# Attention with sinks and a sliding window, then a gated feed-forward layer: sink keys and the neighbouring half tile scored by separate 64-wide matmuls, sink values placed by small DMAs, casts and masks open to several engines

## The chip, the cores and the metric

The kernel runs on one core of one Trainium2 chip. The metric is the device time of one execution in microseconds (us); several executions give a median. Five engines work side by side and meet only through semaphores: PE (TensorE, matmul and transposes), DVE (VectorE), ACT (ScalarE), POOL (GpSimd, which here also issues the loads) and SP (SyncE, which here issues stores, DMA transposes and, in the changed kernel, small copies inside on-chip memory).

## What is computed

Inputs are float32; four batches, eight heads, 768 tokens, 64 features per head. Heads 0, 2 and 6 ("retrieval") attend causally to all earlier tokens. Heads 1, 3, 4, 5 and 7 ("streaming") see only the first four tokens (the sinks) and the last 64.

```python
scores = (1/8) * q @ k.T                       # per batch and head
keep   = causal                                # retrieval heads
keep   = causal & (key < 4 | query - key < 64) # streaming heads
a      = softmax(where(keep, scores, -1e9)); attn = a @ v
x      = attn, heads side by side              # 3072 tokens x 512
h      = gelu(x @ w_gate) * (x @ w_val)        # 512 -> 1536
out    = x + sigmoid(x @ w_res) * (h @ w_out)  # 1536 -> 512
```

## The kernel before

**Chunks.** The 3072 tokens are taken in six chunks of 512 tokens, four query tiles of 128 each. With six tiles to a batch, chunk 0 is tiles 0 to 3 of batch 0; chunk 1 is tiles 4 and 5 of batch 0 with tiles 0 and 1 of batch 1; chunk 2 is tiles 2 to 5 of batch 1; chunks 3, 4 and 5 repeat this for batches 2 and 3. Chunks 1 and 4 therefore handle two short segments with twice as many, but half as wide, casts and evictions. Each chunk runs three steps: `attention`, `gate_value`, `output`. The output of a chunk is interleaved with the attention of the next, so the program alternates between an "attention stage" (attention of chunk c with the output of chunk c-1) and a "gate/value stage" (96 matmuls of 512 columns). The last output stands alone at the end.

**Keys and queries.** They are needed with features on partitions. For batch 0 and for tiles 0 to 5 of batch 1 (chunks 0, 1, 2) `loads_rows` fetches them by large row loads from POOL (L410), transposes them on PE (L504) and evicts them alternately on DVE and ACT (L512) into `qkt`. From chunk 3 on `loads_natural` fetches them in 64 KB pieces into the staging tile `qks` and SP transposes them by DMA (L534). Two heads share 128 partitions, so one matmul has 64 contraction rows, and two heads' matmuls can run beside each other in the two row halves of PE. There are two buffers each of `qks`, `qkt`, `va` and `vs`.

**Sinks.** A streaming head needs, for query tile i, its own tile ("diag"), and of the tile ahead of it only the second half of the keys, plus the four sinks ("prev"). So `key_sinks` (L459 to L474) makes a copy `kts` of the keys of each tile (L465), then overwrites its first four columns by the sink keys (L468); `values` makes the same copy `vs` of the values (L449) and overwrites its first four rows (L452). All four copies are DVE work. One matmul of 128 keys by 128 queries then scores sinks and window together (L602, `kts` operand), and one weighs both (L668, `vs` operand).

**Attention.** Per pair of heads: `scores` (L602) fills PSUM banks `pb` of 512 columns; `exps` takes the exponential on ACT (L613) into `er` or `es` and multiplies masks `m_causal`, `m_diag`, `m_prev` on DVE (L641); `weigh` multiplies by the values (L668; a column of ones gives the sum), takes the reciprocal (L675) and normalises into `xtok` (L678), both DVE. When both heads of a group of 128 features (`cb`) are done, `to_features` casts it to 16 bits on DVE (L689), transposes it on PE (L693) and evicts it on DVE (L697) into `xT`.

**Gate, value, output.** `gate_value` makes 12 groups of 4 + 4 matmuls over the four `cb` (L731); every one of them depends on all of `xT`. ACT takes the gelu (L735), DVE forms h (L737). `output` makes, for each of four token tiles, 4 matmuls by `wr` (L753), 12 by `wo` (L758), a tanh on ACT (L761, in place of the sigmoid), a multiply on DVE (L763), an add of x on POOL (L767; on DVE in the last chunk) and a store on SP (L773). ACT holds either the exponential's or the gelu's table and loads it anew at each change (ACT_TABLE_LOAD).

**What sets the order.** The kernel's Python holds a list of tasks with an engine, an estimated duration, dependencies and a priority (1000 per chunk, then offsets). `Graph.schedule` (L122) simulates the engines with these estimates and fixes each engine's order for good: at each moment a free engine takes its ready task of lowest priority number. `assign_waits` and `emit` turn the dependencies into semaphores. Engines then work strictly in that order, so a late task holds back what stands behind it on its engine. PSUM has eight banks: two for weighted values, six shared by scores (`scr`, at most 4) and feed-forward (`moe`, at most 4).

## Time and profile before

| what | value |
|---|---|
| median of 3 runs | 323.49 us (321.61 to 324.11) |
| the profiled execution | 323.42 us, of which the span of the profile is 321.7 |
| TensorE clock granted, mean | 0.963 of full |
| busy: PE, DVE, ACT, POOL | 283.0, 177.9, 141.8, 106.2 us |
| matmuls | 2096, 88% of the span busy |
| gelu / exponential table loads | 12 of some 1.28 us |

The span is a single profiled execution from its first to its last instruction; what lies around it is 1.7 us. A row of the grouped view reads: line of the kernel, engine, operation, written tile <- read tiles, shapes, number of times | busy us, mean ns of one | idle time of the engine just ahead of them and what ended it. A row of the chain of waits reads: start, duration, engine, tile and line; it follows the work that ended last back from the end. A row of the stage table reads: stretch in us, its length, then busy time and number of instructions of PE, of its weight loads (PEld), of DVE, ACT and POOL, then the granted PE clock, the DMA share and GB/s. Matmul durations overlap, since they are pipelined; spacing between starts says more than the duration of one.

### The profile page before, as it was taken

Reading aid. Unit: us, or ns where it says so; the run is one execution under the profiler, and the core shown is the slowest. Engines: PE = TensorE matmul, PEld = TensorE weight load, DVE = VectorE, ACT = ScalarE, POOL = GpSimd, SP = SyncE. Lnnn points to the kernel's source line nnn. Section 1 sums busy time; section 2 is a strip of 40 time slices with the busy share of each in tenths; the row PEclk is TensorE's granted clock in tenths of the full one; section 3 lists DMA queues with packets and bytes.
Section 4 is the critical chain, followed back from the end, with each engine's and each line's share of the span. In section 5 each row is a group of like instructions: output and inputs, shape, how many; then the busy total and the mean of one; then the engine's idle time right before and its main releaser. Section 6 shows DMA issues by size and latency. Waiting matters only on the chain.

```text
span 321.7 us, 5361 instructions
## 1 busy us (share of the span) xinstructions
PE 283.0 (88%) x2096; PEld 137.4 (43%) x2096; DVE 177.9 (55%) x474; ACT 141.8 (44%) x256; POOL 106.2 (33%) x128
## 2 busy tenths in 40 slices
PE   1476999799999999499999899998499999699994
PEld 1254344354444455234445444454144445344442
DVE  0888336768674458824568734278623416924333
ACT  2336253952633768023576233864023578223310
POOL 8979302947662531795011300110300012100000
PEclk9999999899999999879999999999579999989999
DMA  9999999999499913799004400010100000100011
GB/s 91 117 194 203 173 202 181 158 61 93 140 120 79 63 65 77 92 141 151 3 3 103 125 0 3 0 67 1 67 0 0 0 35 35 65 0 2 0 56 75
DMA packets 80488, 24.46 MB, mean 76 GB/s; under 512 B 68176, under 2 KB 77392, under 8 KB 80464
## 3 DMA queue, kind: packets, MB, share of 16 engines
q0 software_dynamic: 63952, 14.69, 50.3%
q1 hardware_dynamic: 16512, 9.44, 11.5%
q8 instruction: 16, 0.26, 0.4%
q14 instruction: 8, 0.07, 0.1%
HBM read 29.36 MB, written 6.29 MB: 111 GB/s over the span
## 4 chain that ended last, share of the span: by engine, by line
PE 81%; DVE 13%; DMA 2%; ACT 2%; issue 1%; POOL 0%; POOLq 0%; DVEq 0%
PE pb L731 41%; PE pb L758 19%; PE pb L753 7%; PE pb L602 5%; PE pb L668 4%; DVE x L689 3%; DVE xtok L678 2%; PE pb L504 2%; PE pb L693 2%; DMA qks<-in_k_dram 2%; DVE es L641 1%; DVE xT L697 1%; DVE otile L763 1%; DVE rcp L675 1%; DVE kts L465 1%
## 5 line engine op out<-in xcount | busy, mean ns | idle before, releaser
L737 DVE SCALAR_TENSOR_TENSOR hT<-gact,pb 128x512 f16<-128x512 f16 x72 | 49.5, 687 | 79.4 <-PE pb L731 77.2
L735 ACT ACTIVATE gact<-pb 128x512 f16<-128x512 f32 x72 | 43.0, 597 | 114.0 <-PE pb L731 113.8
L731 PE MATMUL pb<-xT,wg 128*128 128x512 f16 x288 | 79.2, 400 | 2.9 <-DVE xT L697 2.9
L731 PE MATMUL pb<-xT,wv 128*128 128x512 f16 x288 | 76.6, 390 | 0.0
L758 PE MATMUL pb<-wo,hT 128*128 128x512 f16 x288 | 73.1, 380 | 0.0
L767 POOL TENSOR_TENSOR otile<-otile,xtok 128x512 f32<-128x512 f32 x20 | 26.2, 1316 | 130.1 <-DVE otile L763 125.9
L731 PEld LDWEIGHTS pb<-xT,wg 128*128 128x128 f16 x288 | 28.4, 101 | 38.8 <-issue 5.3
L731 PEld LDWEIGHTS pb<-xT,wv 128*128 128x128 f16 x288 | 29.0, 101 | 36.7 <-issue 5.4
L613 ACT ACTIVATE er<-pb 128x512 f16<-128x512 f32 (+2 forms) x72 | 34.9, 550 | 11.5 <-PE pb L602 11.4
L613 ACT ACTIVATE es<-pb 128x512 f16<-128x512 f32 (+1 forms) x60 | 30.6, 563 | 18.7 <-PE pb L602 17.0
L758 PEld LDWEIGHTS pb<-wo,hT 128*128 128x128 f16 x288 | 24.0, 98 | 24.5 <-issue 2.2
L763 DVE SCALAR_TENSOR_TENSOR otile<-srs,pb 128x512 f32<-128x512 f32 x24 | 16.3, 679 | 26.0 <-PE pb L758 17.7
L410 POOL DMA_DIRECT2D qks<-in_q_dram x29 | 23.1, 827 | 16.5 <-PE pb L504 16.1
L410 POOL DMA_DIRECT2D qks<-in_k_dram x29 | 22.9, 812 | 15.6 <-PE pb L504 9.9
L753 PE MATMUL pb<-wr,xT 128*128 128x512 f16 x96 | 25.5, 391 | 0.0
L410 POOL DMA_DIRECT2D va<-in_v_dram x24 | 21.6, 914 | 10.4 <-PE pb L668 10.4
L602 PE MATMUL pb<-qkt 64*128 64x128 f16 (+3 forms) x276 | 22.7, 256 | 2.2 <-DVE qkt L512 1.1
L761 ACT ACTIVATE srs<-pb 128x512 f32<-128x512 f32 x24 | 14.4, 601 | 20.3 <-PE pb L753 13.0
L693 PE MATMUL pb<-ident,x 128*128 128x128 f16 x96 | 11.9, 243 | 12.9 <-DVE x L689 12.9
L678 DVE TENSOR_TENSOR xtok<-pb,rcp 128x256 f32<-128x256 f32 (+1 forms) x64 | 21.4, 348 | 0.3
L668 PE MATMUL pb<-va,er 128*128 128x65 f16 x252 | 14.7, 200 | 4.5 <-DVE er L641 3.5
L675 DVE RECIPROCAL rcp<-pb 128x4 f32<-128x4 f32 (+1 forms) x64 | 10.6, 171 | 13.0 <-PE pb L668 12.2
(44 smaller groups left out, 251.5 us busy)
## 6 DMA issues: line engine op xcount, KB each, us to landing
out_dram<-otile SPq DMA_DIRECT2D x24, 256.0 KB, 2.0
va<-in_v_dram POOLq DMA_DIRECT2D x24, 128.0 KB, 6.6
wg<-in_moe_w_gate_dram POOLq DMA_DIRECT2D x3, 512.0 KB, 9.8
wv<-in_moe_w_val_dram POOLq DMA_DIRECT2D x3, 512.0 KB, 11.5
wo<-in_moe_w_out_dram POOLq DMA_DIRECT2D x4, 384.0 KB, 20.2
qks<-in_k_dram POOLq DMA_DIRECT2D x24, 64.0 KB, 4.4
qks<-in_q_dram POOLq DMA_DIRECT2D x24, 64.0 KB, 4.2
qks<-in_q_dram POOLq DMA_DIRECT2D x4, 256.0 KB, 10.5
```

Source lines behind the costliest of these rows:

```text
L410: return G.add(eng, issue, lambda e: e.dma_start(out_ap(), in_ap), deps, prio, bufs=bufs, dma=cost, name=name, grp=grp)
L602: out_.append(e.matmul(at(scr)[:, o:o + nq * 128], lhsT=src, rhs=at(BB.qkt)[half, 0, q0:q0 + nq, p, :], start=True, stop=True))
L613: tx = G.add("act", c_act(cols), lambda e: e.activation(out=at(et)[:, off:off + cols], in_=at(scr)[:, 0:cols], func=AF.Exp, scale=SM_SCALE ...
L668: r.append(e.matmul(at(av)[:, (i - a) * 65:(i - a) * 65 + 65], lhsT=at(et)[:, pos:pos + 128], rhs=val, start=(i == a and y == 0), stop=(y ...
L678: t2 = G.add("dve", c_dve(n * 64), lambda e: e.tensor_tensor(out=at(xbuf)[:, lt0:lt0 + n, h * 64:(h + 1) * 64], in0=at(av)[:, 0:n * 65].re ...
L731: return lambda e: [e.matmul(at(dst)[:, :], lhsT=w[:, ci, f * 128:(f + 1) * 128], rhs=at(xtbuf)[:, ci, :], start=(ci == 0), stop=(ci == NC ...
L735: ta = G.add("act", c_act(512), (lambda gb=gb, ga=ga: lambda e: e.activation(out=at(ga)[:, :], in_=at(gb)[:, :], func=AF.Gelu))(), [tg], p ...
L737: th = G.add("dve", c_dve(512), (lambda vb=vb, ga=ga, f=f: lambda e: e.scalar_tensor_tensor(out=at(h)[:, f, :], in0=at(ga)[:, :], scalar=0 ...
L753: e.matmul(at(rb)[:, :], lhsT=at(xtbuf)[:, ci, s], rhs=wr[:, ci, :], start=(ci == 0), stop=(ci == NCB - 1))
L758: e.matmul(at(fb)[:, :], lhsT=at(h)[:, fi, s], rhs=wo[:, fi, :], start=(fi == 0), stop=(fi == NF - 1))
L763: t1 = G.add("dve", c_dve(512), (lambda fb=fb, sr=sr, ot=ot: lambda e: e.scalar_tensor_tensor(out=at(ot)[:, :], in0=at(sr)[:, :], scalar=1 ...
L767: t2 = G.add(on, 0.6 if on == "dve" else 1.3, (lambda ot=ot, lt=lt: lambda e: e.tensor_tensor(out=at(ot)[:, :], in0=at(ot)[:, :], in1=at(x ...
```

## The change

Six things are done together.

1. **Scores of the prev tile without key copies.** `kts`, its buffers and `key_sinks` are gone. For each bank one 64-wide matmul of keys 0 to 63 of tile 0 scores the sinks for all of the bank's prev queries into PSUM partitions 0 to 63, and one 64-wide matmul per query tile scores keys 64 to 127 of the tile ahead into partitions 64 to 127. So 100 matmuls of 128 keys become 140 of 64 keys. The mask stays.
2. **Sink values by DMA.** Rows 0 to 63 of `vs` are zeroed once; SP places the four sink rows (L481 of the new kernel, 4 DMAs) and rows 64 to 127 (L489, 12 DMAs), in place of 28 DVE copies.
3. **Casts, masks, evictions on any free engine.** `Graph.flex` gives a task alternatives; the scheduler takes the engine that its estimates say is done first, and fixes it. As it comes out: masks 77 on DVE and 27 on POOL; casts of x 17 on ACT, 10 on POOL, 5 on DVE (32 on DVE before); evictions of `xT` 23 on ACT, 9 on DVE (32 on DVE before); evictions of transposed q and k 17 on ACT, 7 on DVE (16 and 16 before).
4. **Gate and value in halves.** The first two `cb` of a group can be multiplied once those two are in `xT`; the halves come after all scores of the chunk. The `moe` cap of banks goes from 4 to 5.
5. **Tables and clock.** The gelu table is loaded right behind the chunk's last exponential, the exponential's at the start of the kernel, each by an activation of one column; 90 matmuls of the identity with itself fill PE in chunk 0 where the scheduler sees it free.
6. **Start and loads.** The masks are built 128 or 256 wide on POOL and spread to full width by DVE or ACT. Chunk 2's q and k now come by 16 more small POOL loads (in place of two large ones) and 8 more DMA transposes on SP, in place of 64 PE transposes. Some duration estimates of the scheduler are changed.

The output of the last chunk is untouched. The core of the diff:

```diff
+ROWS_UNTIL = 2
...
+BIAS = {"act": 0.2, "dve": 0.5, "pool": 0.0}
...
+                    if t.alts and any(max(free[f], now) + t.alts[f][0] + BIAS[f] < now + t.alts[e][0] + BIAS[e] - 1e-6
+                                      for f in t.alts if f != e):
+                        continue
...
-    P_ps = Pool(banks[2:8], caps={"moe": 4, "scr": 4})
+    P_ps = Pool(banks[2:8], caps={"moe": 5, "scr": 4})
...
+            BB.vsink = G.add("sp", 1.2, lambda e: e.dma_start(
+                at(BB.vs)[0:N_SINK, :, :, :].rearrange("p i h d -> p i (h d)"),
+                at(BB.v)[0:N_SINK, 0:1, :, :].rearrange("p i h d -> p i (h d)").to_broadcast(
+                    [N_SINK, NT - 1, NHEAD * (DHEAD + 1)])),
+                [BB.vtok[0]], base + 1, bufs=[BB.v, BB.vs], dma=0.1, name="vsink")
...
+            t = G.add("sp", 1.2, (lambda lo=lo, hi=hi: lambda e: e.dma_start(
+                at(BB.vs)[64:128, lo:hi, :, :].rearrange("p i h d -> p (i h d)"),
+                at(BB.v)[64:128, lo:hi, :, :].rearrange("p i h d -> p (i h d)")))(),
...
-        base = 1000 * (c - 2) + 50
+        base = -15 if c == 1 else 1000 * (c - 2) + 50
...
+                if s:
+                    if bi == 0 or not blocks[bi - 1][0]:
+                        w = sum(1 for y in blocks if y[0])
+                        deps.append(BB.ktok[p, 0])
+                        put((0,), slice(0, 64), (0, slice(0, 64)), o, q0, w)
+                    put((1,), slice(64, 128), (kt, slice(64, 128)), o, q0, 1)
+                else:
+                    put((0, 1), slice(0, 128), (kt, slice(0, 128)), o, q0, nq)
...
-            tm = G.add("dve", c_dve(w * 128, 1.5, False),
+            tm = G.flex({"dve": (c_dve(w * 128, 1.4, False), fm), "pool": (c_pool(w * 128, 0.55), fm)}, [tx, mt], pr,
+                        bufs=[et], name=f"mask{S_.h}")
...
+        tc_ = G.flex({"dve": (c_dve(n * 128, 1.2, False), cast("dve")), "act": (c_act(n * 128), cast("act")),
+                      "pool": (c_pool(n * 128), cast("pool"))},
...
+        te = G.flex({"dve": (c_dve(n * 128, 1.8), ev("dve")), "act": (c_act(n * 128), ev("act"))},
+                    [tp], pr - 3, bufs=[scr, xtbuf], name="xE")
...
+            for c0 in (0, 2):
+                xd = [t for cb, t in xttoks if c0 <= cb < c0 + 2]
+                tg = G.add("pe", c_mm(512, 2), mk(wg, gb, c0), xd + [wtok["g", f // 4], tg], pr, bufs=[gb, xtbuf], order=last_sc[c], name=f"g{f}")
+                tv = G.add("pe", c_mm(512, 2), mk(wv, vb, c0), xd + [wtok["v", f // 4], tv], pr, bufs=[vb, xtbuf], order=last_sc[c], name=f"v{f}")
...
+    warm = Buf(P_ps, "warm")
+    for _ in range(90):
+        G.add("pe", 0.11, lambda e: e.matmul(at(warm)[:, 0:128], lhsT=ident[:, :], rhs=ident[:, :], start=True, stop=True),
+              [t_ident], 1e9, bufs=[warm], name="warm")
...
-            (loads_rows if c < 3 else loads_natural)(c, si, b, a, z)
+            (loads_rows if c < ROWS_UNTIL else loads_natural)(c, si, b, a, z)
```

**PE and ACT where chunk 2's attention passes into its gate/value stage.** A row is an instruction with its line, tiles and shape; x3 is three more of it; in brackets what it waits for (cnt_dve: a count kept by DVE). On PE before, the end of the attention is the last weighting of values, two transposes of x, then the gate matmuls, four to a group:

```order
L668 MATMUL pb<-vs,es 128x65
L668 MATMUL pb<-va,es 128x65
L693 MATMUL pb<-ident,x 128x128 [waits cnt_dve]
L693 MATMUL pb<-ident,x 128x128 x3
L693 MATMUL pb<-ident,x 128x128 [waits cnt_dve]
L693 MATMUL pb<-ident,x 128x128 x3
L731 MATMUL pb<-xT,wg 128x512 [waits cnt_dve]
L731 MATMUL pb<-xT,wg 128x512 x3
L731 MATMUL pb<-xT,wv 128x512 x4
```

On PE now, at the same place:

```order
L719 MATMUL pb<-ident,x 128x128 [waits cnt_act]
L719 MATMUL pb<-ident,x 128x128 x3
L793 MATMUL pb<-wo,hT 128x512 x3
L763 MATMUL pb<-xT,wg 128x512 [waits cnt_dve,cnt_act]
L763 MATMUL pb<-xT,wg 128x512
L763 MATMUL pb<-xT,wv 128x512 [waits cnt_act]
L763 MATMUL pb<-xT,wv 128x512
L689 MATMUL pb<-vs,es 128x65 [waits cnt_dve]
...
L763 MATMUL pb<-xT,wg 128x512 x2
...
L763 MATMUL pb<-xT,wv 128x512 x2
L719 MATMUL pb<-ident,x 128x128 [waits cnt_act,cnt_dve]
L719 MATMUL pb<-ident,x 128x128 x3
```

Half groups of gate and value (two matmuls) now stand between the weighting of the last heads and ahead of the third transpose; two more stand between the third and the fourth. Ten matmuls of 512 columns lie ahead of the last transpose, where none lay. ACT before, around the same moment:

```order
L613 ACTIVATE es<-pb 128x512 [waits cnt_pe]
L613 ACTIVATE es<-pb 128x512
L761 ACTIVATE srs<-pb 128x512
L735 ACT_TABLE_LOAD
L735 ACTIVATE gact<-pb 128x512 [waits cnt_pe] x3
```

ACT now:

```order
L713 ACTIVATE x<-xtok 128x512 [waits cnt_dve] x2
L633 ACTIVATE es<-pb 128x512 [waits cnt_pe]
L633 ACTIVATE es<-pb 128x512
L726 ACTIVATE xT<-pb 128x512 [waits cnt_pe]
L633 ACTIVATE es<-pb 128x512 x2
L756 ACT_TABLE_LOAD
L756 ACTIVATE scratch<-ident 128x1
L796 ACTIVATE srs<-pb 128x512
L713 ACTIVATE x<-xtok 128x512 [waits cnt_dve]
L726 ACTIVATE xT<-pb 128x512 [waits cnt_pe] x2
L770 ACTIVATE gact<-pb 128x512 [waits cnt_pe] x12
```

Three casts and three evictions of this chunk's x came to ACT; two casts and one eviction stand ahead of the last exponentials, and the gelu's table load stands ahead of the last cast.

**POOL during chunk 1.** Before, the small loads of chunk 3 and its values come in one run, then the adds of chunk 0's output:

```order
L410 DMA qks<-in_k_dram 128x4x64 [waits cnt_pe]
L410 DMA qks<-in_k_dram 128x4x64
L410 DMA qks<-in_q_dram 128x4x64 x2
...
L410 DMA va<-in_v_dram 128x8x64 [waits cnt_pe]
L410 DMA va<-in_v_dram 128x8x64 x5
L767 TENSOR_TENSOR otile<-otile,xtok 128x512 [waits cnt_dve] x4
```

Now:

```order
L661 TENSOR_TENSOR es<-es,m_diag 128x256 [waits cnt_act]
L661 TENSOR_TENSOR es<-es,m_prev 128x256 [waits cnt_act]
L444 DMA qks<-in_k_dram 128x4x64
L713 CAST x<-xtok 128x256 [waits cnt_dve]
L444 DMA qks<-in_q_dram 128x4x64 x2
...
L661 TENSOR_TENSOR es<-es,m_prev 128x128 [waits cnt_act] x2
L444 DMA va<-in_v_dram 128x8x64 [waits cnt_pe]
L444 DMA va<-in_v_dram 128x8x64 x3
L661 TENSOR_TENSOR es<-es,m_diag 128x256 [waits cnt_act]
L661 TENSOR_TENSOR es<-es,m_prev 128x128 [waits cnt_act]
L801 TENSOR_TENSOR otile<-otile,xtok 128x512 x2
```

Masks and casts of the running chunk stand between the loads of later chunks, so a load waits for a mask's exponential, and a mask for a buffer that a load waits for.

**SP, first stores.** Before, the first rows of SP:

```order
L773 DMA out_dram<-otile 128x512 [waits cnt_pool] x4
L534 DMA_TRANSPOSE qkt<-qks 128x4x128 [waits dma_154]
L534 DMA_TRANSPOSE qkt<-qks 128x4x128 [waits dma_157]
...
L534 DMA_TRANSPOSE qkt<-qks 128x4x128 [waits dma_181]
L773 DMA out_dram<-otile 128x512 [waits cnt_pool] x2
```

Now, behind ten copies of values:

```order
L489 DMA vs<-va 64x1560 [waits dma_201,dma_200,dma_199]
L554 DMA_TRANSPOSE qkt<-qks 128x4x128 [waits dma_150,dma_149,dma_193]
...
L554 DMA_TRANSPOSE qkt<-qks 128x4x128 [waits cnt_pe,dma_222]
...
L554 DMA_TRANSPOSE qkt<-qks 128x4x128 [waits dma_249]
L807 DMA out_dram<-otile 128x512 [waits cnt_pool]
L481 DMA vs<-va 4x5x520 [waits dma_228]
```

Sixteen DMA transposes (chunk 2's and chunk 3's) now stand ahead of the first store, where the four stores of chunk 0 came first.

More of the change, by code (lines that the diff above doesn't have):

```diff
@@ L120, in add, with flex @@
         return t
+    def flex(self, alts, deps, prio, **k):
+        eng = next(iter(alts))
+        t = self.add(eng, alts[eng][0], alts[eng][1], deps, prio, **k)
+        t.alts = alts
+        return t
     def schedule(self):
@@ L597, in sc @@
-        def sc(e):
-            out_ = []
-            for (x, scr, o, s, kt, q0, nq) in mms:
-                half = slice(64 * x, 64 * x + 64)
-                src = at(BB.kts)[half, kt, p, :] if s else at(BB.qkt)[half, 1, kt, p, :]
-                out_.append(e.matmul(at(scr)[:, o:o + nq * 128], lhsT=src, rhs=at(BB.qkt)[half, 0, q0:q0 + nq, p, :],
-                                     start=True, stop=True))
-            return out_
-        dur = max(sum(c_mm(m[6] * 128) for m in seq) for seq in seqs)
@@ L606, in scores, with put @@
-        ts = G.add("pe", dur, sc, deps, pr, bufs=scrs + [BB.qkt, BB.kts], order=chunk_xt[c - 1] + [near_end.get(c - 1)], name=f"sc{p}")
+            o, lanes = 0, [0, 0]
+            half = slice(64 * x, 64 * x + 64)
+            def put(cols, rows, keys, o, q0, nq):
+                at_ = max(lanes[y] for y in cols)
+                for y in cols:
+                    lanes[y] = at_ + nq
+                mms.append((at_, len(mms), half, scr, rows, keys, o, q0, nq))
+            blocks = S_.packs[r]
@@ new lines, in scores @@
+            dur = max(dur, max(lanes))
+        mms.sort(key=lambda m: m[0:2])
+        def sc(e):
+            return [e.matmul(at(scr)[rows, o:o + nq * 128], lhsT=at(BB.qkt)[half, 1, kt, p, ks],
+                             rhs=at(BB.qkt)[half, 0, q0:q0 + nq, p, :], start=True, stop=True)
+                    for (_, _, half, scr, rows, (kt, ks), o, q0, nq) in mms]
+        ts = G.add("pe", c_mm(128, dur), sc, deps, pr, bufs=scrs + [BB.qkt], order=chunk_xt[c - 1] + [near_end.get(c - 1)],
+                   name=f"sc{p}")
@@ L725, in gate_value @@
         toks = []
+        G.add("act", 0.2, lambda e: e.activation(out=scratch[:, :], in_=ident[:, 0:1], func=AF.Gelu), [t_ident],
+              1000 * c - 100, fset="gelu", order=exps_of[c], name="table")
         for f in range(NF):
```

186 lines of the change are left out of this document (88 added, 98 removed).

## The prediction

> **What bounds the kernel now.** I read the page first, then the stages, then the gaps between them. On the page: span, busy times, the granted clock in 40 slices, and the chain of waits by engine and by line.
>
> ```profile
> span 321.7 us, 5361 instructions
> PE 283.0 (88%) x2096; PEld 137.4 (43%) x2096; DVE 177.9 (55%) x474; ACT 141.8 (44%) x256; POOL 106.2 (33%) x128
> PEclk9999999899999999879999999999579999989999
> PE 81%; DVE 13%; DMA 2%; ACT 2%; issue 1%; POOL 0%; POOLq 0%; DVEq 0%
> PE pb L731 41%; PE pb L758 19%; PE pb L753 7%; PE pb L602 5%; PE pb L668 4%; DVE x L689 3%; DVE xtok L678 2%; PE pb L504 2%; PE pb L693 2%; DMA qks<-in_k_dram 2%; DVE es L641 1%; DVE xT L697 1%; DVE otile L763 1%; DVE rcp L675 1%; DVE kts L465 1%
> ```
>
> PE is the bound: 81% of the chain. DVE holds 13%, split over casts, normalisations, masks and evictions; the key copies that the change removes appear with 1%. The clock dips three times, near 0.5 once. The stage table shows where: rows alternate between attention (chunk c with the output of c-1) and gate/value, after chunk 0 and its gate/value.
>
> ```profile
> 0.00:32.90 32.90, 16.48 (x202) 11.30 (x203) 20.87 (x57) 13.40 (x25) 29.64 (x44) 1.00 1.18 152
> 32.90:56.70 23.80, 23.80 (x157) 10.91 (x158) 10.98 (x27) 9.00 (x20) 4.38 (x6) 1.00 1.73 186
> 56.70:83.60 26.90, 23.52 (x224) 12.31 (x223) 21.30 (x95) 14.55 (x29) 18.77 (x24) 0.94 1.28 102
> 83.60:107.20 23.60, 23.60 (x166) 11.19 (x165) 12.01 (x24) 10.36 (x18) 13.47 (x18) 1.00 0.93 112
> 107.20:135.70 28.50, 23.92 (x243) 12.14 (x243) 20.77 (x50) 17.18 (x31) 10.66 (x11) 0.97 0.48 70
> 135.70:159.10 23.40, 23.40 (x98) 10.00 (x100) 8.77 (x15) 7.35 (x13) 13.85 (x19) 0.89 1.43 107
> 159.10:180.70 21.60, 20.75 (x202) 10.60 (x201) 16.85 (x45) 13.45 (x25) 4.61 (x4) 1.00 0.29 66
> 180.70:201.60 20.90, 20.89 (x98) 9.39 (x100) 8.78 (x13) 7.37 (x13) 0.63 (x1) 1.00 0.09 23
> 201.60:231.20 29.60, 23.50 (x224) 11.67 (x224) 20.36 (x79) 15.05 (x28) 5.10 (x4) 0.92 0.08 29
> 231.20:254.70 23.50, 23.50 (x100) 10.06 (x102) 7.57 (x11) 7.42 (x13) 0.00 (x0) 0.89 0.03 10
> 254.70:281.70 27.00, 23.74 (x242) 11.97 (x240) 15.85 (x42) 17.12 (x31) 5.06 (x4) 0.98 0.11 40
> 281.70:303.80 22.10, 22.10 (x97) 9.80 (x98) 7.56 (x11) 7.16 (x12) 0.00 (x0) 0.94 0.00 1
> 303.80:321.70 17.90, 13.84 (x65) 6.08 (x62) 6.21 (x9) 2.39 (x4) 0.00 (x0) 1.00 0.15 59
> ```
>
> Chunk 3 (159.10 to 201.60) needs 21.6 + 20.9 = 42.5 us at full clock. Chunks 1, 2, 4 and 5 take 50.5, 51.9, 53.1 and 49.1. Their attention holds more matmuls than chunk 3's 202: 22 more (1 and 4), 41 more (2 and 5). What such a matmul costs stands in the chain (start, duration, engine, line):
>
> ```profile
> 119.30 0.67 PE pb L668 x22
> 203.12 1.29 PE pb L758 x6
> 89.70 1.01 PE pb L504 x32
> 32.87 11.59 PE pb L731 x48
> 177.47 0.41 PE pb L668 x13
> 179.95 0.72 DVE xT L697 x2
> 131.89 1.14 DVE kts L465
> ```
>
> 22 weightings take 0.67 us, 30 ns each; scores are wider. At 36 ns, 22 more are 0.8 us; 41 more, with more of the wide scores, are 1.8 at 43 ns. By chunk 3's measure, then, the four would take 43.3, 44.3, 43.3, 44.3: they lose 7.2 + 7.6 + 9.8 + 4.8 = **29.4 us**. Of these 2.0 are two blocks of transposes in chunk 1 (1.01 each). The rest is at and behind the boundaries, as 4-us windows around two of them show (same columns):
>
> ```profile
> 132.00:136.00 4.00, 0.94 (x6) 0.47 (x6) 3.44 (x5) 0.00 (x0) 3.99 (x6) 0.76 1.18 116
> 136.00:140.00 4.00, 4.00 (x11) 1.44 (x10) 0.62 (x1) 0.60 (x1) 4.00 (x6) 0.50 1.89 132
> 228.00:232.00 4.00, 1.61 (x6) 0.54 (x7) 2.63 (x6) 0.00 (x0) 1.26 (x1) 0.50 0.34 131
> ```
>
> PE nearly stops while five or six DVE instructions fill the window, and then runs at clock 0.50 although it is busy throughout. Each gap is paid twice. The instructions in the second gap, DVE and POOL apart, then PE:
>
> ```profile
> 223.59 0.28 DVE L689 CAST x<-xtok 128x256 f16<-128x256 f32 x1
> 226.80 1.25 DVE L689 CAST x<-xtok 128x256 f16<-128x256 f32 x1
> 226.64 1.26 POOL L767 TENSOR_TENSOR otile<-otile,xtok 128x512 f32<-128x512 f32 x1 [12.20 <-DVE otile L763]
> 230.39 0.40 PE L693 MATMUL pb<-ident,x 128*128 128x128 f16 x2 [1.89 <-DVE x L689]
> ```
>
> The same cast takes 0.28 us alone and 1.25 beside a POOL add, nearly the add's length, and PE waits 1.89 us for such a cast.
>
> In sentences that the rest does not need: the Trainium skill, "SBUF — State Buffer", section "Who interferes with whom", says that DVE copies and casts in a two-port mode, and DVE instructions with two inputs in SBUF, share a port pair with GpSimd under an exclusive lock, and whoever comes second blocks entirely. The trace agrees, 1.25 against 0.28. It speaks for moving casts to ACT and against new tensor work on POOL, which is rival C.
>
> **The change part by part.** The sum is made against the profiled span 321.7; the execution itself took 323.42, so 1.7 us lie around it, and the median of the runs is 323.49, practically the same.
>
> *Start and chunk 0 (56.7 us with its gate/value).* DVE early, SP's transposes later, and rows by form (last: ns of one):
>
> ```profile
> 11.50 1.85 DVE L468 COPY kts<-qkt 128x16 f16<-128x16 f16 x1
> 87.06 10.64 SPq L534 DMA_TRANSPOSE qkt<-qks  x8
> L452 DVE COPY vs<-va 4x520 f16<-4x520 f16 x11 | 7.4, 672 | 0.2
> L767 POOL TENSOR_TENSOR otile<-otile,xtok 128x512 f32<-128x512 f32 x20 | 26.2, 1316 | 130.1 <-DVE otile L763 125.9 <-DVE rcp L675 4.2
> L512 ACT ACTIVATE qkt<-pb 128x512 f16<-128x512 f16 x8 | 4.3, 600 | 7.3 <-PE pb L504 7.3
> L512 ACT ACTIVATE qkt<-pb 128x256 f16<-128x256 f16 x8 | 2.4, 390 | 1.0 <-PE pb L504 1.0
> 119.90 0.40 PE L602 MATMUL pb<-qkt,kts 64*128 64x128 f16 x8
> ```
>
> A copy of 16 columns held DVE for 1.85 us ahead of the first mask; it goes, with the copies around it: -2.5 (between 0, if the mask itself is then late, and -2.6). Half groups of gate and value fill the end of the attention, ten matmuls of 215 ns (1.29 / 6): -2.2 (0 to -2.2). The first 48 gate/value matmuls took 241 ns each; PE kept busy should give them 215: -1.2 (0 to -1.2). Against this, 57 of the 90 warm-up matmuls stand between real work; at a quarter of 215 ns each they cost 0 to 3.1, and I take 0, since PE was busy for only 16.48 of 32.90 us there. Values now reach `vs` by SP instead of a 0.67 us copy; not shown in the trace, so bounded by 0 and, as SP work, by its 1.33 us transposes (10.64 / 8); the last streaming heads need them late: 0. Sum -5.9, so **50.8** (47 to 54).
>
> *Scores.* 100 matmuls become 140, with 20 pairs of banks. The sinks and windows of a bank can run beside each other in the column halves, so the price is at least 0. The row of eight gives 0.40 us for eight, with the next instruction 0.33 behind the first: 41 ns each, 1.6 us for 40 more. If the halves don't overlap at all, the prev part doubles: 50 pair steps of 54 ns, 2.7. I put it into the per-chunk term below.
>
> Again apart from the sum: the Trainium skill, "TensorEngine Tiling (Array Packing)", section "Key Properties", says that a change of tiling mode drains the TensorE. The eight-matmul step, 0.33 us against four pair steps of 54 ns, leaves 0.11 for switches; by that rule 20 banks' switches would make the sum some 2 us longer, 292.
>
> *The boundaries of chunks 1 to 5.* Casts of x leave DVE in 27 of 32 cases and evictions in 23, copies leave entirely, and ten half-group matmuls (2.2 us) stand where PE waited. Even chunk 3 has a gap: from 177.88 to 180.67, 2.8 us of DVE work, of which the halves can cover 2.2; as PE's rows stand they do so only where the first two groups of features are ready: -1.5 per chunk (0 to -2.2). With no gap of several us, the half clock goes too, as it is absent in chunk 3. What stands against it: 37 new tensor instructions on POOL (27 masks, 10 casts), six per chunk. The trace has no such mask or cast on POOL. The bounds are 0.28 (on DVE) and 1.32 (the add, wider and of float32); nearest is half an add, some 0.7, plus what it blocks on DVE. Put a quarter of them on the path at 1.0 us: +1.5 per chunk, scores included (0 to +7.8, if all six are on the path at 1.3). So **42.5** per chunk remains, chunk 3's present time, plus 0.8 + 1.8 + 0 + 0.8 + 1.8 for size: 5 x 42.5 + 5.2 = 217.7.
>
> *ACT.* 17 casts (6 of 256, 11 of 512) and 23 evictions (11 and 12) come to it: 17 x 0.39 + 23 x 0.60 = 20.4 us; no ACT cast from on-chip memory is in the trace, so I take the PSUM rows, which may be 0.2 too long or too short. Spread over six chunks this is 3.4 each: in chunks 2 and 5 ACT rises from 17.2 to 20.6, as much as PE needs there (21.6 - 2.8 + 1.8 = 20.6). Its exponentials stand behind casts, and PE's scores behind exponentials: +1 each (0 to +3), **+2.0**.
>
> *Hidden edits.* Chunk 2's transposes are worth the 2.0 counted above. Their 16 loads move onto POOL's queue, and 8 transposes onto SP's, where now 16 (21 us) stand ahead of chunk 0's stores; cover is the time of chunk 1, some 43 us; without it the three `otile` buffers run out and PE's output matmuls wait. The table preloads keep the 12 table loads and only shift them; both sides 1.3 us per chunk, I take 0.
>
> *Sum:* 50.8 + 217.7 + 2.0 + 17.9 (last output, untouched) = 288.4; with 1.7 around it **290 us**, 33 less than before.
>
> **The rivals.**
>
> *A. New waits take the place of the old.* The cast no longer stops at a POOL add, but ACT or POOL is late where DVE was; a mask on POOL between loads, or a cast behind the last exponentials. Half of the 27.4 us of gaps and half clock stays: 288.4 + 13.7 + 1.7 = **304**. For it: ACT's 20.6 us in chunks 2 and 5. Against it: DVE had 3.44 of 4.00 us in a gap, ACT 0.00.
>
> *B. Everything fits.* No lock and no ACT wait: 288.4 - 7.5 - 2.0 + 1.7 = **281**. For it: chunk 3 shows full clock even with a gap.
>
> *C. POOL and DVE block each other* (the other side). The 37 POOL instructions are in the attention stages, beside 77 masks on DVE; each that holds PE costs its whole length. It decides from 33.3 / 37 = 0.9 us each; at the add's 1.3, 288.4 + 48.1 - 7.5 + 1.7 = **331**, slower. For it: 1.25 against 0.28. Against it: the adds are 20 longer instructions, and only those at a boundary held PE up.
>
> *D. Early transfers are late.* `vs` copies, 16 more loads or the stores behind 16 transposes eat the gain of the start: 290 + 6 = **296**. For it: a DMA share over 1 until 83.6.
>
> *E. The change doesn't do what it says*: the copies were hidden, and moves only shift waits. Only the 1% of the key copies returns: 323.4 - 3.2 = **320**.
>
> **How the numbers follow.** Forecast 0.57; A 0.17, B 0.13, C 0.03, D 0.07, E 0.03. About 1% (3.2 us) is what a measurement can tell from no change. Faster by over 1%: the forecast, A, B and D, 0.94; E is within 1%, 0.03; slower C, 0.03. The forecast's own range is 282 to 298: chunk 0 gives -3.8 to +3.2, ACT -2 to +4, the boundaries -3.5 (the halves' last 0.7 each) to some +1 each. To hold 8 in 10 I reach to A and B with a little of their own spread: 276 to 306.
>
> **What would show it.** Right: chunk 0 with its gate/value ends at 47 to 54 us; no slice of the clock row below 0.8 after the first; each chunk's pair of stages 42 to 46; DVE busy falls to some 120 to 135, ACT rises to some 162; casts on ACT near 0.6 us; no mask over 0.7 us in the chain more than a few times. Wrong: gaps of over 2 us at the boundaries ending on ACT `xT` or POOL `es` (A); POOL masks with DVE masks over 1 us beside them on the chain (C); PE waiting for `vs` or `qkt` (D). The forecast itself falls if clock dips remain in two or more boundaries.

## The result, and the profile after

The changed kernel takes **306.03 us** (median of 304.34, 304.98, 307.09 and 308.17) against 323.39 before: a ratio of 0.947 (0.940 to 0.955), 17 us faster where 33 were forecast, and just outside the stated range. The profiled execution is the fastest of the four, 304.34 us, with a span of 302.3. For every run, the time given is the median of all its executions, while ratios and intervals leave out executions over 1.5% slower than the fastest of the same kernel. The page of the changed kernel:

```profile
span 302.3 us, 5444 instructions
PE 279.0 (92%) x2162; PEld 136.3 (45%) x2162; DVE 143.3 (47%) x332; ACT 162.1 (54%) x305; POOL 136.8 (45%) x179
PEclk9999999999699999999999999999999999999999
PE 81%; DMA 6%; DVE 5%; POOL 5%; ACT 1%; issue 1%; POOLq 0%; DVEq 0%
```

DVE fell from 13% to 5% of the chain, POOL rose from 0% to 5%, and ACT is busy for the 162 us that were worked out. DVE's busy time, 143.3 us, did not fall to the 120 to 135 that the prediction named. One clock dip is left, near 80 us. By chunk, from the end of one gate/value stage to the end of the next (columns as in the stage table; the last row is the last output):

```profile
0.00:51.70 51.70, 42.30 (x460) 24.55 (x462) 25.19 (x54) 29.34 (x60) 42.06 (x65) 1.00 1.42 178
51.70:103.80 52.10, 46.14 (x330) 21.68 (x332) 28.32 (x73) 26.25 (x52) 36.39 (x48) 0.93 1.93 163
103.80:150.30 46.50, 45.12 (x345) 21.37 (x346) 20.69 (x47) 27.76 (x51) 22.17 (x26) 1.00 1.06 105
150.30:190.50 40.20, 39.76 (x292) 19.03 (x292) 19.09 (x41) 23.64 (x44) 9.02 (x9) 1.00 0.06 21
190.50:238.00 47.50, 46.81 (x343) 22.15 (x342) 24.03 (x65) 25.21 (x49) 16.87 (x24) 1.00 0.08 29
238.00:284.40 46.40, 45.08 (x344) 21.49 (x344) 19.75 (x43) 27.31 (x50) 10.24 (x9) 1.00 0.06 24
284.40:302.30 17.90, 13.79 (x64) 6.07 (x62) 6.21 (x9) 2.57 (x5) 0.00 (x0) 1.00 0.15 59
```

The forecast had 50.8, 43.3, 45.3, 42.5, 43.3, 45.3 and 17.9 (ACT's 2.0 in the third and sixth). Twelve matmuls by `wo`, 2.6 us, moved from chunk 3's stage into chunk 4's, so read 42.8 and 44.9 there. **Chunk 1 is 8.8 us over and even slower than before (49.7, by the same borders); chunks 2, 4 and 5 are 1.1 to 1.6 over.** Where chunk 1 loses it, in 4-us windows:

```profile
71.70:75.70 4.00, 2.69 (x21) 1.28 (x19) 4.00 (x11) 3.34 (x7) 4.00 (x6) 1.00 1.76 123
75.70:79.70 4.00, 0.70 (x5) 0.20 (x5) 4.00 (x4) 0.00 (x0) 4.00 (x5) 0.69 2.11 149
79.70:83.70 4.00, 3.26 (x14) 1.36 (x14) 1.54 (x8) 1.14 (x3) 4.00 (x6) 0.50 1.64 161
```

PE is all but idle while four DVE instructions fill 4 us, then the clock is at 0.50: the gap of before, paid twice again. The instructions in it (DVE, POOL, PE):

```profile
74.29 1.37 DVE L661 TENSOR_TENSOR er<-er,m_causal 128x256 f16<-128x256 f16 x1
75.58 2.88 DVE L661 TENSOR_TENSOR es<-es,m_prev 128x128 f16<-128x128 f16 x1
78.47 1.28 DVE L661 TENSOR_TENSOR es<-es,m_diag 128x256 f16<-128x256 f16 x1
71.18 3.59 POOL L444 DMA_DIRECT2D va<-in_v_dram  x4 [2.62 <-PE pb L689]
74.75 0.72 POOL L661 TENSOR_TENSOR es<-es,m_diag 128x256 f16<-128x256 f16 x1
75.91 3.69 POOL L801 TENSOR_TENSOR otile<-otile,xtok 128x512 f32<-128x512 f32 x3
80.09 0.21 PE L689 MATMUL pb<-va,es 128*128 128x65 f16 x1 [3.68 <-DVE rcp L696]
```

A mask of 128 columns takes 2.88 us beside three adds that POOL does in one run. DVE had finished what these adds need at 59.4, 64.6 and 70.4 us; POOL came to them at 75.91, behind masks and loads, among them a load of values that waits for PE (2.62 us). **Theory 1** is this order; **theory 2** the transfers (SP's sixteen transposes ahead of the stores, POOL's extra loads); **theory 4** came from the score steps (below); theory 3 is named at its one run.

### The profile page after: what moved, and what is told of

Read it like the earlier page. It is cut to its first block, busy times and chain, and to the rows that moved or that the text cites. A ratio compares the mean times of both kernels' runs of the same rounds, so it can differ in the third digit from the quotient of the medians.

```text
span 302.3 us, 5444 instructions
## 1 busy us (share of the span) xinstructions
PE 279.0 (92%) x2162; PEld 136.3 (45%) x2162; DVE 143.3 (47%) x332; ACT 162.1 (54%) x305; POOL 136.8 (45%) x179
## 4 chain that ended last, share of the span: by engine, by line
PE 81%; DMA 6%; DVE 5%; POOL 5%; ACT 1%; issue 1%; POOLq 0%; DVEq 0%
PE pb L763 38%; PE pb L793 21%; PE pb L621 7%; PE pb L788 7%; DMA qks<-in_q_dram 6%; PE pb L689 4%; PE pb L719 2%; DVE es L661 1%; POOL va L444 1%; ACT xT L726 1%; POOL qks L444 1%; DVE x L713 1%; DVE xtok L699 1%; PE pb L524 1%; POOL wg L444 1%
## 5 line engine op out<-in xcount | busy, mean ns | idle before, releaser
L763 PE MATMUL pb<-xT,wg 128*128 128x512 f16 x288 | 86.3, 381 | 3.5 <-ACT xT L726 2.5
L763 PE MATMUL pb<-xT,wv 128*128 128x512 f16 x288 | 85.6, 383 | 0.2 <-DMA wv<-in_moe_w_val_dram 0.2
L801 POOL TENSOR_TENSOR otile<-otile,xtok 128x512 f32<-128x512 f32 x20 | 25.4, 1273 | 67.9 <-DVE otile L798 65.4
L763 PEld LDWEIGHTS pb<-xT,wv 128*128 128x128 f16 x288 | 27.8, 98 | 33.2 <-issue 0.6
L763 PEld LDWEIGHTS pb<-xT,wg 128*128 128x128 f16 x288 | 26.3, 98 | 35.0 <-ACT xT L726 4.6
L444 POOL DMA_DIRECT2D qks<-in_k_dram x36 | 28.4, 816 | 13.4 <-PE pb L524 8.6
L621 PE MATMUL pb<-qkt 64*128 64x128 f16 (+6 forms) x416 | 30.1, 244 | 0.0
L444 POOL DMA_DIRECT2D qks<-in_q_dram x36 | 28.4, 820 | 0.3 <-POOL ident L415 0.3
L661 POOL TENSOR_TENSOR es<-es,m_diag 128x256 f16<-128x256 f16 (+1 forms) x14 | 11.9, 858 | 29.8 <-ACT es L633 29.8
L621 PEld LDWEIGHTS pb<-qkt 64*128 64x128 f16 (+1 forms) x416 | 13.9, 97 | 18.2 <-issue 6.2
```

What stands on the lines that cost most here:

```text
L444: return G.add(eng, issue, lambda e: e.dma_start(out_ap(), in_ap), deps, prio, bufs=bufs, dma=cost, name=name, grp=grp)
L621: return [e.matmul(at(scr)[rows, o:o + nq * 128], lhsT=at(BB.qkt)[half, 1, kt, p, ks], rhs=at(BB.qkt)[half, 0, q0:q0 + nq, p, :], start=Tr ...
L661: fm = lambda e, o0=off + o, w=w, msk=msk: e.tensor_tensor(out=at(et)[:, o0:o0 + w * 128].rearrange("p (i k) -> p i k", k=128), in0=at(et) ...
L763: return lambda e: [e.matmul(at(dst)[:, :], lhsT=w[:, ci, f * 128:(f + 1) * 128], rhs=at(xtbuf)[:, ci, :], start=(ci == 0), stop=(ci == NC ...
L801: fa = lambda e, ot=ot, lt=lt: e.tensor_tensor(out=at(ot)[:, :], in0=at(ot)[:, :], in1=at(xbuf)[:, lt, :], op=ALU.add)
```

## The experiments

Moves in the fixed orders are made behind `G.schedule()`, in the lists of tasks by engine; nothing else moves in those runs. "Planned anew" means that the scheduler chose all orders again. Times are medians beside runs of the kernel before on the same chip; the ratio is to these, with its interval. A chunk's length is that of the one profiled execution, and chunk 0 varies by some us from execution to execution (see the next section), so the length of chunk 1 and the later ones says more about an edit than the median. Diffs are excerpts.

**e1_adds_early.** Adds where they are ready:

```diff
+    pool.insert(pool.index(m[1]) + 1, a[0])
+    pool.insert(pool.index(m[2]), a[1])
+    pool.insert(pool.index(m[3]) + 1, a[2])
```

> The changed kernel with one edit: the first three of chunk 0's four output adds, which POOL reaches only at 75.9 us, behind loads and masks, stand where they are ready in POOL's fixed order (behind the second, ahead of the third and behind the fourth of chunk 1's masks on POOL). Nothing else moves. Theory 1 (lock): at the end of chunk 1's attention these three adds, 3.7 us in one run, hold up DVE masks (2.88, 1.37 and 1.28 us against some 0.3), PE idles 3.7 + 1.1 us and then runs at half clock; with the adds gone from there chunk 1 falls from 52.1 to some 45 and the time from 306 to 299 to 301. Theory 2 (late transfers: SP's sixteen transposes ahead of the stores, POOL's extra loads): SP's order and the loads are as before, so the time stays within 1.5 us of 306.

302.02 us, 0.934 (0.929 to 0.939). The 128-column mask of 2.88 us falls to 0.21, but chunk 1 only from 52.1 to 50.2. What is late now (DVE, POOL, PE):

```profile
74.59 0.21 DVE L680 TENSOR_TENSOR es<-es,m_prev 128x128 f16<-128x128 f16 x1
72.16 3.59 POOL L463 DMA_DIRECT2D va<-in_v_dram  x4
75.72 0.72 POOL L680 TENSOR_TENSOR es<-es,m_diag 128x256 f16<-128x256 f16 x1
76.50 0.20 PE L708 MATMUL pb<-va,es 128*128 128x65 f16 x1 [0.96 <-POOL es L680]
```

The blocked mask was theory 1's, but chunk 1 gave back 1.9 us where some 7 were expected: a mask on POOL, behind four loads, is next.

**f1_adds_masks_early.** These two masks ahead of the loads as well:

```diff
+    i = pool.index(a[2]) + 1
+    pool[i:i] = m[4:6]
```

> The run with the three adds in their places, and also the last two of chunk 1's masks on POOL, which stood behind four loads of values (3.6 us), placed ahead of these loads. Theory 1, widened (not the lock alone but POOL's fixed order: whatever PE needs from POOL waits behind what POOL waits for): PE's wait of 0.96 us for such a mask goes, and with it the half clock at 79 to 84 us; chunk 1 from 50.2 to 46 or 47, the time from 302.0 to 298 or 299. Theory 2 (transfers): the stay of chunk 1 at 50 is due to something else and nothing is won: 301 to 303.

302.35 us, 0.932 (0.924 to 0.940): no gain over the run before, and chunk 1 at 52.5, against theory 1 as widened. The gap at the boundary is gone, the clock stays 1.00 there, and the time is lost later. PE's longest wait (total, times, longest), then SP:

```profile
PE pb L782 <- DVE otile L817: 5.0, 1, 5.0
```

```profile
56.68 27.28 SPq L573 DMA_TRANSPOSE qkt<-qks  x16
84.00 0.60 SPq L826 DMA_DIRECT2D out_dram<-otile  x1
```

The fourth output's multiply finds no free `otile`, since the first store stands behind sixteen transposes.

**h1_stores_early.** The first three stores ahead of chunk 3's transposes, too:

```diff
+    i = sp.index(dt[8])
+    sp[i:i] = outs
```

> The run with adds and masks early, and on SP the first three stores of chunk 0 placed between chunk 2's eight DMA transposes and chunk 3's eight. Theory 2, in its place: with POOL's order mended PE waits 5.0 us in chunk 1's gate/value stage, because the fourth output finds no free otile until SP has done sixteen transposes (56.7 to 84.0 us); with the stores ahead of the last eight the wait goes, chunk 1 falls from 52.6 to 46 to 48, the time from 302.4 to 297 or 298. If the wait has another cause it stays at 302.

298.39 us, 0.926 (0.920 to 0.932). As expected; chunk 1 takes 45.9:

```profile
53.20:99.10 45.90, 44.68 (x333) 21.23 (x334) 24.62 (x73) 26.25 (x52) 34.75 (x46) 1.00 1.97 156
```

**s0_stores_only.** The SP edit alone.

> The changed kernel with the three stores ahead of chunk 3's transposes on SP and POOL's order as it was. Theory 1 (POOL's order alone makes the gap): the adds come at 76 to 80 us as before, so the gap stays and the time is 306 within 1.5. Theory 2 alone (SP's transposes are the cause): chunk 1 falls by 4 or more, 301 to 302.

306.52 us, 0.948 (0.939 to 0.957): nothing; chunk 1 stays at 52.1. The stall at SP exists only once POOL's is gone. Both queues together cost chunk 1 6.2 us, and neither alone gives them back.

**e3_rows3.** `ROWS_UNTIL = 3`.

> The changed kernel with chunk 2's q and k loaded by rows and transposed on PE again, as before the change (two large loads in place of 16, 64 PE transposes in place of 8 DMA transposes); planned anew. Theory 2 (late transfers): without 16 loads on POOL and 8 transposes ahead of the stores chunk 1 falls by 5 us or more, less the 2 us for PE transposes: 300 to 303. Theory 1 (lock): the loads matter only in that they delay the adds, so part of the gap may go too; if adds still come in a burst at a boundary 306 to 309, and the trace tells by whether a DVE mask over 1 us stands beside them.

302.59 us, 0.936 (0.931 to 0.942), chunk 1 at 49.4: fewer loads on POOL and transposes on SP give back 2.7 us of it, from the same two queues. The adds no longer come in one run here: POOL does them at 63.19, 66.99, 77.97 and 80.67 us, and one DVE mask of 1.26 us still stands beside the third.

**e2_masks_dve.** `{"dve": ..., "pool": ...}` of the masks becomes `{"dve": ...}`.

> The changed kernel with all masks on DVE (the 27 that POOL took go back); the order is planned anew. Theory 1 (lock between POOL tensor work and DVE): POOL is freer, the adds run when ready, chunk 1's gap closes: 298 to 302. Theory 3 (the masks on POOL are a real relief for DVE): slower than 306, 308 or more. Theory 2 (late transfers): 306.

305.93 us, 0.949 (0.943 to 0.954). Chunk 1 falls to 46.6, as theory 1 has it, while the later chunks rise by 0.2 to 1.3, 2.6 in all, as theory 3 has it. Chunk 0 is 3.5 us longer at a lower clock, but DVE and POOL have the same 54 and 65 instructions there in both kernels, so no mask moved in it; run s0, with chunk 0's orders unchanged, has the same 55.2 us. In this execution chunk 0 thus hides the gain in chunk 1.

**e4_wide_prev.** One 128-wide matmul for prev; the sinks are left out:

```diff
-                        put((0,), slice(0, 64), (0, slice(0, 64)), o, q0, w)
-                    put((1,), slice(64, 128), (kt, slice(64, 128)), o, q0, 1)
+                    put((0, 1), slice(0, 128), (kt, slice(0, 128)), o, q0, 1)
```

> The changed kernel with the prev tile scored by one 128-wide matmul of the keys of the tile ahead, and the sink keys left out (so that part of the computation is not done: 100 matmuls of 128 keys stand in place of 140 of 64). All orders are the same. Theory 4 (64-wide scores are dearer than the forecast's 0.3 us per chunk): score steps take 0.6 to 1.3 us less per chunk, 4 to 5 us in all, 301 to 303. If 64-wide matmuls cost only 41 ns each as more of the same: 1.6 us, 304.5.

302.55 us, 0.939 (0.932 to 0.946). Chunks 1 to 5 take 1.4, 0.6, 0.6, 1.2 and 0.6 us less than in the changed kernel. Two kinds of score step must be told apart. In the first, both heads are streaming, and each has a full bank of prev scores: two sink matmuls of 512 columns and eight window matmuls of 128. The changed kernel, then the same step in this run, each with the next instruction:

```profile
116.51 0.42 PE L621 MATMUL pb<-qkt 64*64 64x512 f16 x10
116.86 0.82 PE L793 MATMUL pb<-wo,hT 128*128 128x512 f16 x3
```

```profile
118.10 0.40 PE L620 MATMUL pb<-qkt 64*128 64x128 f16 x8
118.43 0.82 PE L792 MATMUL pb<-wo,hT 128*128 128x512 f16 x3
```

From start to start 0.35 against 0.33 us: sinks and windows run beside each other, and the extra matmuls cost 0.02. In the second kind one head is streaming and the other (heads 4 and 6 form such a pair) is a retrieval head with 512 columns of 128 keys. Again the changed kernel, then this run:

```profile
118.69 1.00 PE L621 MATMUL pb<-qkt 64*64 64x512 f16 x6
119.62 0.60 PE L793 MATMUL pb<-wo,hT 128*128 128x512 f16 x2
```

```profile
120.27 0.39 PE L620 MATMUL pb<-qkt 64*128 64x128 f16 x5
120.60 0.61 PE L792 MATMUL pb<-wo,hT 128*128 128x512 f16 x2
```

From start to start 0.93 against 0.33 us. Inside the first of these steps the sink matmul and one window start at 118.69; then come the retrieval head's matmul of 128 keys and the other three windows:

```profile
119.02 0.39 PE L621 MATMUL pb<-qkt 64*128 64x512 f16 x1
119.34 0.35 PE L621 MATMUL pb<-qkt 64*64 64x128 f16 x3
```

The three starts lie 0.33 and 0.32 us apart, and a matmul of 512 columns takes 0.215; so matmuls of 64 and of 128 keys stand one after the other here, and each change from one kind to the other adds some 0.11 us (an estimate from these spacings). In this run, where all have 128 keys, the two heads run beside each other, in 0.33 us. Added up over all score steps from start to next start, the changed kernel takes 1.37, 0.65, 0.65, 1.26 and 0.65 us more in chunks 1 to 5, which is the difference of the chunks within 0.1; steps of 64-key matmuls alone have 0.05 or less of it in any chunk. Theory 4 holds, and its place is the step that mixes both kinds. No run put a step's 64-key matmuls together, ahead of or behind the others, so what that would save was not measured.

**g3_before_scores.** The kernel before with parts 1 and 2 of the change alone (the changed `scores` and `values`, no `key_sinks`).

> The kernel before with the first two parts of the change alone: 64-wide scores, no key copies, sink values by DMA from SP; planned anew. The forecast's view (copies worth some 5 us of the chain, scores 0.3 us per chunk): 317 to 320. Theory 4 (the 64-wide scores cost 0.6 to 1.4 us per chunk, some 5 us, and eat what the copies gave back): 321 to 325.

326.21 us, 1.009 (1.005 to 1.013): slower by 0.9%. In the profiled executions chunk 0 takes 2.3 us less than before (57.5 to 55.2) and chunks 1 to 5 together 4.9 more, near the 4.6 us that the score steps cost in the changed kernel. The scores cost more than the copies gave back.

**i1_key_copies.** The reverse: the changed kernel with `key_sinks` and the `scores` of before.

> The changed kernel with the first part undone: key copies on DVE and 128-wide prev scores as before, all else as changed; planned anew. Theory 4 (64-wide scores cost 4 to 5 us of PE and the relieved DVE has room for the copies): faster than the changed kernel, 301 to 304. If the copies are what crowded DVE: 306 to 312.

299.52 us, 0.927 (0.919 to 0.934): faster than the changed kernel by 6.5 us, more than expected. Between the profiled executions it is 4.5: chunks 2 to 5 take 3.2 less, and their score steps are as long as in e4, while chunk 1 stays at 52.2 and chunk 0 takes 1.4 less.

**g1_before_casts_act.** The kernel before with casts and evictions on ACT or DVE:

```diff
-        tc_ = G.add("dve", c_dve(n * 128, 1.5, False), ...
+        tc_ = G.flex({"dve": (c_dve(n * 128, 1.2, False), cast("dve")), "act": (c_act(n * 128), cast("act"))},
```

> The kernel before with the casts of x and the evictions of xT free to run on ACT or DVE (not POOL) and nothing else of the change; planned anew. If the boundary gaps of before were the casts held by POOL's adds on DVE, as the forecast has it, they should shrink to the size of chunk 3's: chunks 2, 4 and 5 together some 12 to 18 us shorter, 305 to 312. If ACT takes DVE's place (rival A of the forecast): 316 to 323.

315.26 us, 0.972 (0.964 to 0.980). Between the two: chunk 4 from 53.1 to 46.1 and chunk 2 from 51.9 to 49.0, chunk 5 none. PE's waits, before and here:

```profile
PE pb L693 <- DVE x L689: 12.9, 12, 2.5
```

```profile
PE pb L719 <- ACT x L714: 6.2, 8, 1.4
```

Half of the wait for casts goes. The longest that is left, 1.4 us, does not come from exponentials ahead of the cast: ACT itself waits there, 1.16 us, for DVE's normalisation into `xtok`.

**g2_before_halves.** The kernel before with half groups.

```diff
+            for c0 in (0, 2):
+                xd = [t for cb, t in xttoks if c0 <= cb < c0 + 2]
```

> The kernel before with gate and value in halves and the cap of five banks, nothing else; planned anew. If filling the gaps is what matters, up to 2.2 us per boundary and the half clock behind it: 308 to 314. If the casts on DVE stay the limit and the halves only run earlier: 316 to 322.

319.38 us, 0.986 (0.979 to 0.993): in the second of the two ranges, with the casts still on DVE.

**e5_no_halves.** The changed kernel with whole groups: `for c0 in (0,)`, all of `xT`.

> The changed kernel with gate and value in whole groups again, each waiting for all of xT; planned anew. The forecast gave the halves 1.5 us per boundary and 2.2 in chunk 0, some 10 us: 314 to 318, gaps of 2 to 3 us at each boundary and some half clock behind them. If the shift of casts and evictions to ACT already closes the gaps: 307 to 310.

315.42 us, 0.972 (0.964 to 0.980): by the medians the halves are worth 9.4 us here, 3.4 in the kernel before. Between the profiled executions it is 11.4, of which 7.3 in chunks 1 to 5 and 4.1 in chunk 0, where this execution has a stop and a low clock (55.8 us at 0.88) that are not shown to come from the edit. That the halves pay more once the casts are early is a reading of the 9.4 against the 3.4; no run shows it alone.

**e6_no_warm.** The warm-up matmuls left out of PE's list.

> The changed kernel without the 90 warm-up matmuls; all other orders the same. If they hold the clock in chunk 0: the first 48 gate/value matmuls run at half clock again, 1.2 us or more slower, 307 to 310. If those that stand between real work only delay it (up to 3.1 us): 303 to 305.

306.32 us, 0.951 (0.942 to 0.960): no difference that can be measured.

**j1_both, j2_both, j3_both.** Key copies (as in i1, planned anew) and chunk 1's orders mended (on SP as in h1; on POOL the three adds, the last cast and two masks ahead of the loads of values), with the key copies placed later on DVE in three steps:

```diff
+    for pr in (1050, 2050, 3050, 4050):
+        first = next(t for t in dve if t.name == "h0" and t.prio == pr + 450)
+        ks = [t for t in dve[:dve.index(first)] if t.name in ("ks", "ksf") and t.prio == pr]
```

(j1: the first of these only; j2: the first two.)

> The changed kernel with key copies and 128-wide prev scores as before (as in the run with key copies), and in chunk 1 these moves in the fixed orders: POOL's three adds and its last cast and two masks ahead of the loads of values, chunk 2's two key copies on DVE behind chunk 1's attention (they stood in it, and DVE idled 3.98 us for SP's transposes), the first three stores on SP ahead of chunk 3's transposes. Theory 1 + 2 + 4, that these are the two wrong terms of the forecast and that they add up: chunk 1 from 52.2 to 45 or 46 and the time from 299.5 to 292 to 294, next to the forecast of 290. If a third cause of several us is left, chunk 1 stays above 48 and the time at 296 or more.

> The run that joined key copies and mended orders, with chunk 3's two key copies also moved on DVE, from chunk 1's gate/value stage to chunk 2's (DVE waited 9.78 us there for SP's transposes, which now stand behind the stores). Theory 1 + 2 + 4 adding up: chunk 1 from 55.7 to 45 to 47, the time from 304.2 to 293 to 295. A third cause left in chunk 1: over 297.

> The run that joined key copies and mended orders, with the key copies of every later chunk standing on DVE behind the attention of the chunk ahead of it (none waits for a DMA transpose in the middle of another chunk's work). Theory 1 + 2 + 4 adding up: chunk 1 at 46, chunk 2 at 45 to 47, the time 292 to 295. A third cause: over 297.

304.19, 301.38 and 298.84 us; 0.940 (0.934 to 0.946), 0.927 (0.923 to 0.932), 0.920 (0.912 to 0.927). In j1 and j2 a key copy of a later chunk held DVE until SP's transpose landed, in j2 for 8.74 us:

```profile
101.07 0.26 DVE L522 COPY kts<-qkt 128x384 f16<-128x384 f16 x1 [8.74 <-DMA qkt<-qks]
```

j3 has no such wait; its profiled execution, with a span of 293.9, is the quickest of the profiled ones, but its median is not told apart from h1's. Two of its chunks:

```profile
49.20:95.30 46.10, 43.49 (x321) 20.59 (x322) 27.01 (x77) 25.52 (x50) 33.38 (x44) 1.00 1.92 159
95.30:144.40 49.10, 45.94 (x342) 22.24 (x343) 24.88 (x46) 27.53 (x50) 29.46 (x35) 0.97 1.32 129
```

Chunk 1 is where theory 1 and 2 put it; chunk 2 is not the 45 to 47 expected, so the two terms add up only in part (0.947 - 0.920 of 323, some 9 us, of the 7.6 + 6.5 that they give singly). In chunk 2 of j3 PE's only wait over 0.7 us is one for a cast on POOL, and the loads that stand ahead of this cast on POOL had waited for SP's transposes out of `qks`:

```profile
116.45 0.40 PE L758 MATMUL pb<-ident,x 128*128 128x128 f16 x4 [2.24 <-POOL x L752]
105.07 1.49 POOL L464 DMA_DIRECT2D qks<-in_k_dram  x2 [6.16 <-DMA qkt<-qks]
```

These loads go on at 105.07 us, about where i1 has them (105.67), though chunk 1 ended 7.2 us earlier here (95.3 against 102.5): PE got ahead of them. From 115.3 to 119.3 us the clock is 0.69. That this is all of the 3.2 us that chunk 2 takes more than in i1 (45.8) is likely and was not tested.

## Why the prediction was wrong

**The size of the miss.** The span is 302.3 us where the sum had 288.4: chunk 1 has 8.8 of the 13.9 us between them, chunks 2 to 5 have 4.2, chunk 0 has 0.9. The median lies another 1.7 us above the profiled execution.

**The bound and the boundaries were read rightly.** PE waited 12.9 us for casts on DVE before; in the changed kernel 2.5, over ACT, DVE and POOL, the longest 1.2. The dips beyond chunk 1 are gone, chunk 0 took 51.7 us against 50.8 in this execution, and in chunks 1 to 5 the half groups are worth 7.3 us, where 1.5 each were priced.

**The step that failed first is "Hidden edits".** It took chunk 1's 43 us as cover for 16 more loads on POOL and 16 transposes ahead of the stores on SP. The cover was there in time but not in order: POOL's masks and adds stand behind those loads. With both orders mended chunk 1 goes from 52.1 to 45.9. Rival A named a mask on POOL between loads, rival C the lock and rival D the stores; each was priced alone, where the runs show them in series, at one place: the adds came in one run because of the loads, blocked the masks, and hid the store. Of the 8.8 us these orders have 6.2 and the score steps 1.4; 1.2 stay open. The sixteen transposes also took 26.0 us on SP, not 21. That rival A's 304 lies near the result is luck: it let half of the gaps stand at every boundary, where the trace has one gap, in chunk 1.

**The per-chunk term "scores included" was too small.** Its price of 1.6 us for all scores assumed that sinks and windows run beside each other, and they do (0.35 against 0.33 us). Its upper bound of 2.7 assumed that the worst is no such overlap. It left out that 64-key and 128-key matmuls stand mixed in some steps: a full step of a streaming and a retrieval head took 0.93 us in place of 0.33. Chunks 1 to 5 lose 4.6 us by the score steps. The rule that a change of tiling mode drains TensorE (the Trainium skill, "TensorEngine Tiling (Array Packing)", section "Key Properties") was kept apart from the sum at 2 us. The trace agrees with it: the matmuls on either side of a change stand one after the other, and a change costs some 0.11 us beyond them.

**The first part of the change was costed as a gain and is a loss.** The key copies were 1% of the chain, and the forecast said so; alone, their removal with the scores and value copies that it needs makes the kernel 0.9% slower.

**The bound "0 to -1.2" for the clock in chunk 0 left out a loss.** In seven of the profiled executions (e2, e3, e4, e5, h1, j1, j2) PE stops for 0.6 to 2.3 us within chunk 0's scores, with no releaser shown, and the clock falls behind it. A window of 4 us in the changed kernel; two in e4, whose orders are the same; and e4's stop on PE ahead of them:

```profile
20.00:24.00 4.00, 3.79 (x53) 2.27 (x47) 2.46 (x10) 3.93 (x8) 4.00 (x6) 1.00 1.24 205
```

```profile
20.00:24.00 4.00, 3.54 (x37) 2.01 (x35) 1.63 (x5) 4.00 (x10) 4.00 (x6) 0.52 1.25 208
24.00:28.00 4.00, 3.86 (x29) 1.82 (x26) 1.95 (x8) 1.60 (x3) 4.00 (x7) 0.63 1.24 205
```

```profile
18.30 0.61 PE L620 MATMUL pb<-qkt 64*128 64x128 f16 x9 [1.58 <-issue]
```

There chunk 0 ends 3.0 us later (54.7 against 51.7). In s0, whose chunk 0 also has the orders of the changed kernel, PE waits for a copy of values into `vs` at this place, the sign that the prediction gave for rival D, and chunk 0 takes 55.2 us:

```profile
17.10 0.20 PE L708 MATMUL pb<-vs,es 128*128 128x65 f16 x1 [0.59 <-DMA vs<-va]
0.00:55.20 55.20, 48.14 (x458) 26.90 (x460) 25.04 (x54) 29.32 (x60) 41.68 (x65) 0.91 1.50 178
```

All later chunks of s0 are within 0.1 us of the changed kernel's, so the whole difference of the two spans, 305.7 against 302.3, is chunk 0's. The changed kernel's slower two runs, 307.09 and 308.17, have clocks of 0.971 and 0.972 against 0.982 and 0.989 of the others; s0's execution (307.79) has 0.972. That they lost their time in the same place is likely and not shown. What stops PE stays open.

**POOL's price was right for the narrow masks.** A mask of 256 columns was put at some 0.7 us and took 0.694 (nine by `m_diag`); the seven wider ones took 0.99 to 1.16. What they block on DVE, and what they wait behind, was the cost. The text allowed up to 7.8 us per chunk for POOL, but its range let in some 1.

**Three slips in the working.** The border between chunks 0 and 1 before was set at 56.7 us; the last matmul of chunk 0's gate/value stage ends at 57.5, so the sum is 0.8 too low. The bounds listed beside the range of 282 to 298 add up to 281 to 302. Rival C's 0.9 us as the price that decides leaves in the 7.5 us that its 331 takes out; without them it is 1.1.

## What to carry to other kernels

Where orders are fixed ahead, price an edit by what stands behind it on its queue, not by the engine's share of busy time: the same loads, masks, adds and stores cost chunk 1 6.2 us more in one order than in another. Undoing one of two stalls in series shows no gain; before calling a theory false, look for the wait that took its place. A part that removes work from an engine with room to spare can cost more than it saves if it adds work to the one that bounds. When a trace shows a step dearer than its matmuls, look inside the step at the starts: here the price was not in the number of small matmuls but in where they stand among wide ones.

## What the runs showed of the hardware that was not expected

A 128-column DVE mask with both inputs in on-chip memory took 2.88 us beside three POOL adds (3.69 us) and 0.21 without them. Matmuls of 64 keys on the two column halves ran beside each other: two heads' banks with ten matmuls took 0.35 us, where eight of 128 keys took 0.33. Matmuls of 64 and 128 keys mixed in one step did not: 0.93 us against 0.33. Ninety matmuls set in to keep the clock up changed nothing that can be measured (ratio 0.951 without, 0.947 with them).
